# One core, cached attention decode: how P reaches its key partitions before PV

## The chip, the core and the metric

One core of one Trainium2 chip runs the whole program in one launch. The metric is the device time of an execution in microseconds. Beside the timed runs there is one profiled execution, whose trace gives the instructions of each engine: TensorE (PE for matmuls, PEld for its weight loads), VectorE (DVE), ScalarE (ACT), GpSimd (POOL) and SyncE (SP), which issues the DMAs.

## What is computed

Two layers, each an attention block with a cache and a gated feed-forward block, for four tokens (batch 4, one query position). The weights of both layers are the same, and so are the caches.

```
def _A_ref(x, k_cache, v_cache, wq, wo):       # Hq 32, Hkv 8, Sk 4096, Dh 128, D 512
    q = (x @ wq).reshape(B, 1, 32, 128).transpose(0, 2, 1, 3)
    k = jnp.repeat(k_cache, 4, axis=1); v = jnp.repeat(v_cache, 4, axis=1)
    p = softmax(einsum("bhqd,bhkd->bhqk", q, k) * 128 ** -0.5)
    o = einsum("bhqk,bhkd->bhqd", p, v)
    return o.transpose(0, 2, 1, 3).reshape(B, 1, 4096) @ wo
def _B_ref(x, w_gate, w_up, w_down):           # F 1792
    return (sigmoid(x @ w_gate) * (x @ w_up)) @ w_down

x = x + _A_ref(layernorm(x), k_cache, v_cache, wq, wo)
x = x + _B_ref(layernorm(x), w_gate, w_up, w_down)
x = x + _A_ref(...)                            # second layer, as the first
x = x + _B_ref(...)
```

A cache of one batch element and one key/value head is 4096 x 128 bf16, 1 MB; there are 32 of K and 32 of V.

## The kernel before, in words

The unit of work is one (layer, batch, key/value head), with 1 MB of K and 1 MB of V. Two units make a stage, which the code calls g; there are 32 stages, in the order written out in ORDER. The table RET says which K and V stay in SBUF for the second layer. Twelve slots of 1 MB hold K and V; pump() hands the next load to SP's queue whenever a slot is free, in a fixed order (loads). A slot is given back after the last matmul that reads it, so SP's queue waits for TensorE: for the scores (L940) where a K slot is freed, and for PV (L1048) where a V slot is.

The program is written as one list of instructions per engine, in program order. Each instruction carries the semaphore waits that follow from the names it reads and writes. The main loop goes over steps k; step k works on stage sg = k up to its probabilities, and on stage vg = k - 1 for its PV. The order on TensorE within a step is: scores(sg), one wo pair of an earlier stage (do_wo), spread_max(sg), pv of both units of vg, ptrans(sg). Between them stand, at places listed in PLACES, the parts of a batch element's pass: the feed-forward block of layer 0, then layer norm and q of layer 1. DVE transposes K in 32x32 blocks (k_turn, L923) ahead of the scores.

What one stage does around the change:

- scores (L940): 16 matmuls of 512 columns write S in four strips of 32 partitions. A row of S_ps is a head with a part of the keys; 64 of the 128 rows are in use, 512 keys long.
- smax (L956) takes row maxima on DVE, spread_max (L965) brings them to every partition by an fp32 matmul with valid_f as moving operand, and softmax has DVE combine them with a mask (L975, its elementwise output goes to junk and is not used) into one bias per row. ACT then makes the exponentials pe_sb (L983), in bf16, and the row sums.
- ptrans (L1000) turns pe_sb: four matmuls, one for each 128 columns, with pe_sb as weights and 64 selected columns of the identity as moving operand. Keys are then on partitions, but each 32-row strip x of the PSUM tile PT holds, for every a, keys that belong on the partitions of strip a. A matmul with head_f (L1007) sums the row sums, and DVE takes the reciprocal into rden (L1015).
- Sixteen copies (L1032), one for each pair (x, a), each 32 partitions by 64 columns, bring PT into pT_sb on the right partitions. All run on ACT, except that in the last stage half of them run on DVE (L1026).
- pv (L1048): for each unit 32 matmuls with V as 128x128 weights and four columns of pT_sb as moving operand. They come in four groups of eight, one for each x, and a group waits only for the copies of its x.
- normalise (L1080) multiplies by rden; wo_pair (L1098) is 32 matmuls into columns 64 and up of the same PSUM tile O_ps, and DVE adds the result to x (L1112).

There is one buffer each of pe_sb, PT and pT_sb.

Of the kernel before, what the change touches and what calls it, by code (L numbers as in the profile page):

```python
# [5 lines left out]
dt = mybir.dt  # L6
# [179 lines left out]
def bass_interleave_layers__gqa_block_cached__glu_gated_glu__decode_kernel(  # L186
# [17 lines left out]
    P = 128  # L204
# [45 lines left out]
    ident_bf = sbt([P, P], dt.bfloat16, "ident_bf")  # L250
    valid_f = sbt([P, 16 * REP], dt.float32, "valid_f")
    head_f = sbt([P, 2 * REP], dt.float32, "head_f")
    mask_f = sbt([P, 2, 8, REP], dt.bfloat16, "mask_f")
    junk = sbt([P, 16 * REP], dt.bfloat16, "junk")

    row_sb = sbt([P, D], dt.bfloat16, "row")
    x_io = row_sb
# [1 line left out]
    xc_sb = sbt([P, KD, Bn], dt.float32, "xc")  # L259
    sq_sb = sbt([P, KD, Bn], dt.float32, "sq")  # L260
    dn_sb = sq_sb
    newt = sbt([P, 9, Bn], dt.float32, "newt")
    lnsum, lnsq, vpe, nt_a, nt_b, nt_c, nt_y, rs = [newt[:, i, :] for i in range(8)]
    y0i = newt[:, 8, :].bitcast(dt.int32)
    xc_bf = sbt([P, KD, Bn], dt.bfloat16, "xc_bf")
    qT_sb = sbt([P, HQ * Bn], dt.bfloat16, "qT")
    qc_sb = sbt([P, Bn, HKV, NT4, REP], dt.bfloat16, "qc")
    qz_sb = [sbt([P, 2, NT4, 4, REP], dt.bfloat16, f"qz{i}") for i in range(2)]
    oT_sb = [sbt([P, HQ, 2], dt.bfloat16, f"oT{i}") for i in range(2)]
    pe_sb = [sbt([P, 4, P], dt.bfloat16, "pe")] * 2  # L270
    pT_sb = [sbt([P, XJ, 4, 4, REP], dt.bfloat16, "pT")] * 2
    rden_2 = sbt([P, 2, 2 * REP], dt.float32, "rden")
    rden_sb = [rden_2[:, i, :] for i in range(2)]
    pe_f = pe_sb[0].rearrange("p j m -> p (j m)").bitcast(dt.float32)
    iota_f = pe_f[:, 0:P]
    pidx = pe_f[:, P:P + 32]
# [166 lines left out]
    def head_masks():  # L443
        dve(
            lambda e: e.tensor_copy(
                valid_f.rearrange("p (g w) -> p g w", g=4),
                ident_bf.rearrange("p (g w) -> p g w", g=4)[:, :, 0:4 * REP],
            ),
            reads=IDENT,
            writes=["valid"],  # L450
        )
        dve(
            lambda e: e.tensor_tensor(
                half_f[:, :, :], rows_f[:, :, 0, 0:4 * REP], rows_f[:, :, 1, 0:4 * REP], ALU.add
            ),
            writes=["pe0"],
        )
        dve(
            lambda e: e.tensor_reduce(
                head_f.rearrange("p (u h) -> p u h", u=2),  # L460
                half_f.rearrange("p u (a h) -> p u h a", h=REP),
                AX.X,
                ALU.add,
            ),
            reads=["pe0"],
            writes=["head"],
        )
        dve(
            lambda e: e.tensor_scalar(
                mask_f[:, :, :, :],  # L470
                head_f.rearrange("p (u h) -> p u h", u=2).unsqueeze(2).broadcast_to([P, 2, 8, REP]),
                1.0, BIG, op0=ALU.subtract, op1=ALU.mult,
            ),
            reads=["head"],
            writes=["mask"],
        )
        dve(
            lambda e: e.tensor_reduce(rm_sb[0], head_f[:, :], AX.X, ALU.add), reads=["head"], writes=["rm0"]
        )
        dve(  # L480
            lambda e: e.tensor_scalar(rowk_f, rm_sb[0], -exp_scale, None, op0=ALU.mult),
            reads=["rm0"],
            writes=["rowk"],
        )
        dve(
            lambda e: e.tensor_reduce(blk_f, ident_bf.rearrange("p (a c) -> p a c", a=4), AX.X, ALU.add),
            reads=IDENT,
            writes=["blk"],
        )
# [63 lines left out]
    def newton_many(y0, nb):  # L553
        y, yk = y0, "y0i"
        for it, three in enumerate((3.0, 12.0, 768.0)):
            dve(
                (lambda y: lambda e: e.tensor_tensor(nt_a[:, 0:nb], y, y, ALU.mult))(y),
                reads=[yk],
                writes=["nt_a"],
            )  # L560
            dve(
                lambda e: e.tensor_tensor(nt_y[:, 0:nb], nt_a[:, 0:nb], vpe[:, 0:nb], ALU.mult),
                reads=["nt_a", "vpe"],
                writes=["nt_y"],
            )
            z, zk = ((nt_b[:, 0:nb], "nt_b"), (nt_c[:, 0:nb], "nt_c"), (rs[:, 0:nb], "rs"))[it]
            dve(
                (lambda y, z, three: lambda e: e.scalar_tensor_tensor(
                    out=z, in0=nt_y[:, 0:nb], scalar=-three, in1=y, op0=ALU.add, op1=ALU.mult
                ))(y, z, three),  # L570
                reads=[yk, "nt_y"],
                writes=[zk],
            )
            y, yk = z, zk
# [10 lines left out]
    def ln_b_rs(nb):  # L585
# [3 lines left out]
                lnsq[:, 0:nb], M[:, 32:32 + KD * nb].rearrange("p (k b) -> p b k", k=KD), AX.X, ALU.add  # L589
            ),  # L590
            reads=["M1"],
            writes=["lnsq"],
        )
        dve(
            lambda e: e.tensor_scalar(vpe[:, 0:nb], lnsq[:, 0:nb], inv_d, eps, op0=ALU.mult, op1=ALU.add),
            reads=["lnsq"],
            writes=["vpe"],
        )
        dve(
# [361 lines left out]
    def spread_max(g):  # L961
        p = g % 2
        S.inst(
            "pe",
            lambda e: e.matmul(  # L965
                MS[:, 0:16 * REP], lhsT=rm_sb[p].broadcast_to([P, P]), rhs=valid_f[:, :], start=True, stop=True
            ),
            reads=[f"rm{p}", "valid"],
            writes=["MS"],
        )  # L970

    def softmax(g):
        p = g % 2
        dve(
            lambda e: e.tensor_tensor_reduce(  # L975
                junk[:, :], MS[:, 0:16 * REP], mask_f.rearrange("p u n h -> p (u n h)"), rowk_f, BIG,
                ALU.add, ALU.min, nm_sb[p],
            ),
            reads=["MS", "mask", "rowk"],
            writes=["junk", f"nm{p}"],  # L980
        )
        act(
            lambda e: e.activation(  # L983
# [11 lines left out]
    def ptrans(g):  # L995
        p = g % 2
        fns = []
        for j in range(4):
            fns.append(
                (lambda j: lambda e: e.matmul(  # L1000
                    PT[:, j * 64:(j + 1) * 64], lhsT=pe_sb[p][:, j, :], rhs=valid_bf, start=True, stop=True
                ))(j)
            )
        S.group("pe", fns, reads=["pe0"] + IDENT, writes=["PT"])
        S.inst(
            "pe",
# [3 lines left out]
            reads=[f"sm{p}", "head"],  # L1010
            writes=["MS"],
        )
        src = PT[:, 0:256].rearrange("p (j g a h) -> p j g a h", j=4, g=4, h=REP)
        dve(
            lambda e: e.reciprocal(rden_sb[p], MS[:, 64:64 + 2 * REP]),  # L1015
            reads=["MS"],
            writes=[f"rden{p}"],
        )
        late = g == NP - 1
        for x in range(XJ):  # L1020
            for a in range(4):
                dst = pT_sb[p][32 * a:32 * a + 32, x, :, :, :]
                frm = src[32 * x:32 * x + 32, :, :, a, :]
                if late and x % 2:
                    dve(
                        (lambda dst, frm: lambda e: e.tensor_copy(dst, frm))(dst, frm),  # L1026
                        reads=["PT"],
                        writes=[f"pT_{x}" if a == 3 else f"pT_{x}_{a}"],
                    )
                else:  # L1030
                    act(
                        (lambda dst, frm: lambda e: e.activation(dst, frm, ACTF.Copy))(dst, frm),  # L1032
                        reads=["PT"],
                        writes=[f"pT_{x}" if a == 3 else f"pT_{x}_{a}"],
                    )

    def pv(i):
        l, b, u = seq[i]
# [1 line left out]
        p = g % 2  # L1040
        s = where["v", b, u]
        vv = slot[s].rearrange("p (j d) -> p j d", d=DH)
        for x in range(XJ):
            fns = []
            for c in range(2):
                for j in range(4):
                    fns.append(
                        (lambda x, c, j: lambda e: e.matmul(  # L1048
                            O_ps[p][:, ul * REP:(ul + 1) * REP],
                            lhsT=vv[:, x * JG + c * 4 + j, :],  # L1050
                            rhs=pT_sb[p][:, x, j, 2 * ul + c, :],
                            start=(x == 0 and c == 0 and j == 0),
                            stop=(x == XJ - 1 and c == 1 and j == 3),
                        ))(x, c, j)
                    )
            rd = [f"s{s}", f"pT_{x}"] + [f"pT_{x}_{a}" for a in range(3)]
            if ul == 0 and x == 0:
                S.group("pe", fns, reads=rd, writes=[f"O{p}"])
            else:
                S.last_write[f"O{p}"] = S.group("pe", fns, reads=rd)  # L1060
        if l == 1 or not kept("v", i):
            free.append(where.pop(("v", b, u)))

# [9 lines left out]
    def normalise(g):  # L1073
# [4 lines left out]
        held[n, u, c] = (l, b)  # L1078
        dve(
            lambda e: e.tensor_tensor(  # L1080
                oT_sb[n][:, u * REP:(u + 2) * REP, c], O_ps[p][:, 0:2 * REP], rden_sb[p], ALU.mult
            ),
            reads=[f"O{p}", f"rden{p}"],
            writes=[f"oT{n}_{u}_{c}"],
        )

    def wo_pair(g, p):
# [7 lines left out]
        for c in range(KD):  # L1095
            for r in range(2 * REP):
                fns.append(
                    (lambda c, r: lambda e: e.matmul(  # L1098
                        O_ps[p][:, 64 + 2 * c:64 + 2 * c + nb],
                        lhsT=wo_sb[:, u * REP + r, c * P:(c + 1) * P],  # L1100
                        rhs=oT_sb[n][:, u * REP + r, 0:nb],
                        start=(r == 0),
# [1 line left out]
                    ))(c, r)  # L1104
                )
        S.group(
            "pe", fns, reads=[f"oT{n}_{u}_{c}" for c in range(nb)] + [f"wo{u}", f"wo{u + 1}"], writes=[f"O{p}"]
        )
        bs = [b] if pb is None else [b, pb]
        for c, bb in enumerate(bs):  # L1110
# [1 line left out]
                (lambda c, bb: lambda e: e.tensor_tensor(  # L1112
                    xT[:, :, bb],
                    xT[:, :, bb],
                    O_ps[p][:, 64:64 + 2 * KD].rearrange("p (k two) -> p k two", two=2)[:, :, c],
                    ALU.add,
                ))(c, bb),
                reads=[f"x{bb}", f"O{p}"],
                writes=[f"x{bb}"],
            )  # L1120

# [60 lines left out]
    for k, (sg, vg) in enumerate(plan):  # L1182
# [36 lines left out]
        do_steps(k, 6)  # L1219
        if sg is not None:  # L1220
            ptrans(sg)
        do_steps(k, 7)
        if vg is not None and vg in ends:
            close(vg, k)
# [72 lines left out]
```

## Time and profile before

| | |
|---|---|
| median of 3 runs | 326.92 us (325.71 to 328.48) |
| the profiled execution | 326.53 us |
| its span, first to last instruction | 324.7 us |
| mean granted TensorE clock | 0.686 |
| HBM read | 122.95 MB, 379 GB/s over the span |
| ACT copies PT to pT (L1032) | 504, 108.1 us busy |
| matmuls into PT (L1000) | 128, 12.0 us busy |
| PV matmuls (L1048) | 2048, 62.0 us busy |
| V loads | 56 of 1 MB, 11.0 us from issue to landing |
| K loads | 48 of 1 MB, 11.7 us from issue to landing |

How to read it: an engine's busy time says only how much of the span it worked. Lines such as "L1032 ACT ACTIVATE pT<-PT ... x504 | 108.1, 214 | 55.1 <-..." give a group of instructions by source line: output and inputs, shapes, count, busy time in us, mean duration of one in ns, and the engine's idle time before them with what ended it. In a timeline line the first number is the start in us from the start of the span, the second the time from the first start to the last end of the group. "issue" means that an engine stood still without waiting for anything that the profile shows.

### The profile page before, as it was taken

How to read it: one execution, taken by the hardware profiler on the slowest of the kernel's cores; microseconds unless marked ns; L12 is line 12 of the kernel's file. 1: busy time of each engine (PE TensorE's matmuls, PEld its weight loads, DVE VectorE, ACT ScalarE, POOL GpSimd, SP SyncE). 2: the span in 40 equal slices, each digit the busy share in tenths (PEclk: the TensorE clock that was granted, in tenths of full speed). 3: DMA queues.
4: the chain of work that ended last, by engine and by line, in shares of the span. 5: the costliest groups of instructions: out<-in, count | busy, mean ns of one | idle time of the engine just before them, and what ended most of it. 6: DMA issues, size and time to landing. Idle time of an engine off the chain costs nothing.

```text
span 324.7 us, 10428 instructions
## 1 busy us (share of the span) xinstructions
PE 227.0 (70%) x4408; PEld 157.4 (48%) x4408; DVE 188.0 (58%) x441; ACT 145.4 (45%) x600; POOL 12.8 (4%) x36
## 2 busy tenths in 40 slices
PE   1345523008197998768798986799797869878975
PEld 1313312006156465546556564464565646455865
DVE  6387343304656458865647696674886467475243
ACT  1005421205045276655435765543676653377620
POOL 0000000000000010000001000000100000010000
PEclk9999999999996655555765555555655555675555
DMA  7999999999999999999999999999999999999800
GB/s 277 428 422 411 401 404 400 401 386 390 400 406 376 339 376 425 418 422 418 410 370 377 417 424 421 421 388 380 377 421 419 420 422 422 417 416 419 369 18 3
DMA packets 22814, 123.63 MB, mean 381 GB/s; under 512 B 2024, under 2 KB 7920, under 8 KB 8944
## 3 DMA queue, kind: packets, MB, share of 16 engines
q1 hardware_dynamic: 22768, 122.96, 94.1%
q8 instruction: 35, 0.57, 0.7%
q14 instruction: 11, 0.09, 0.1%
HBM read 122.95 MB, written 0.00 MB: 379 GB/s over the span
## 4 chain that ended last, share of the span: by engine, by line
DMA 29%; PE 24%; issue 22%; DVE 12%; SPq 11%; ACT 1%; POOL 0%; DVEq 0%; POOLq 0%
DMA slot<-in_A_v_cache_dram 19%; PE O_ps L1048 7%; DVE slot L923 7%; SPq L382 6%; DMA wo<-in_A_wo_dram 5%; DMA slot<-in_A_k_cache_dram 5%; SPq L368 4%; PE S_ps L940 4%; PE O_ps L1098 3%; PE MS L965 2%; PE MS L1007 2%; PE M_ps L858 1%; DVE small L956 1%; PE M_ps L809 1%; PE PT L1000 1%
## 5 line engine op out<-in xcount | busy, mean ns | idle before, releaser
L1032 ACT ACTIVATE pT<-PT 32x64 bf16<-32x64 f32 x504 | 108.1, 214 | 55.1 <-PE PT L1000 43.6
L923 DVE STREAM_TRANSPOSE slot<-slot 128x2048 f32<-128x2048 f32 (+1 forms) x61 | 112.3, 1840 | 32.4 <-DMA slot<-in_A_k_cache_dram 32.4
L1048 PE MATMUL O_ps<-pT,slot 128*128 128x4 bf16 x2048 | 62.0, 166 | 26.3 <-DMA slot<-in_A_v_cache_dram 26.3
L1048 PEld LDWEIGHTS O_ps<-pT,slot 128*128 128x128 bf16 x2048 | 63.5, 105 | 29.8 <-DMA slot<-in_A_v_cache_dram 27.2
L940 PE MATMUL S_ps<-slot,qz 128*16 128x512 bf16 x512 | 59.4, 612 | 3.4 <-POOL qz L675 2.3
L983 ACT ACTIVATE pe<-S_ps,small 128x512 bf16<-128x512 f32 x32 | 22.0, 686 | 59.0 <-issue 40.4
L965 PE MATMUL MS<-valid_f,small 128*128 128x64 f32 x64 | 20.6, 422 | 22.4 <-DVE small L956 22.4
L1098 PEld LDWEIGHTS O_ps<-oT,wo 128*128 128x128 bf16 x640 | 19.3, 105 | 28.8 <-issue 28.4
L965 PEld LDWEIGHTS MS<-valid_f,small 128*128 128x128 f32 x64 | 15.0, 291 | 37.6 <-DVE small L956 34.1
L1098 PE MATMUL O_ps<-oT,wo 128*128 128x2 bf16 (+1 forms) x640 | 20.3, 166 | 16.7 <-DMA wo<-in_A_wo_dram 15.6
L956 DVE TENSOR_REDUCE small<-S_ps 128x1 f32<-128x512 f32 x32 | 21.2, 662 | 6.5 <-PE S_ps L940 6.5
L675 POOL TENSOR_TENSOR qz<-qc,small 128x128 bf16<-128x128 bf16 x32 | 12.6, 399 | 280.9 <-ACT qc L661 143.5
L940 PEld LDWEIGHTS S_ps<-slot,qz 128*16 128x16 bf16 x512 | 12.4, 109 | 22.8 <-issue 17.7
L1007 PE MATMUL MS<-head_f,small 128*128 128x8 f32 x64 | 17.9, 353 | 0.0
L1080 DVE TENSOR_TENSOR oT<-O_ps,rden 128x8 bf16<-128x8 f32 x32 | 5.2, 164 | 19.7 <-PE O_ps L1048 17.9
L1007 PEld LDWEIGHTS MS<-head_f,small 128*128 128x128 f32 x64 | 16.4, 314 | 0.0
L1015 DVE RECIPROCAL rden<-MS 128x8 f32<-128x8 f32 x32 | 6.6, 206 | 14.8 <-PE MS L1007 14.8
L975 DVE CUSTOM_DVE_ANT_0 junk<-MS,mask_f,small 128x64 bf16<-128x64 f32 x32 | 8.5, 267 | 11.4 <-PE MS L965 11.4
L1000 PE MATMUL PT<-ident_bf,pe 128*128 128x64 bf16 x128 | 12.0, 231 | 1.9 <-ACT pe L983 1.5
L1112 DVE TENSOR_TENSOR xT<-xT,O_ps 128x4 f32<-128x4 f32 x32 | 3.9, 154 | 16.1 <-PE O_ps L1098 16.0
L809 PE MATMUL M_ps<-wq,xc_bf 128*1 128x512 bf16 x128 | 12.9, 574 | 0.0
L661 ACT ACTIVATE qc<-M_ps 128x128 bf16<-128x128 f32 x8 | 1.9, 280 | 19.5 <-PE M_ps L650 19.5
(79 smaller groups left out, 150.3 us busy)
## 6 DMA issues: line engine op xcount, KB each, us to landing
slot<-in_A_v_cache_dram SPq DMA_DIRECT2D x56, 1024.0 KB, 11.0
slot<-in_A_k_cache_dram SPq DMA_DIRECT2D x48, 1024.0 KB, 11.7
wq<-in_A_wq_dram SPq DMA_DIRECT2D x4, 1024.0 KB, 7.8
wo<-in_A_wo_dram SPq DMA_DIRECT2D x8, 512.0 KB, 15.9
wg<-in_B_w_gate_dram SPq DMA_DIRECT2D x4, 448.0 KB, 14.0
wu<-in_B_w_up_dram SPq DMA_DIRECT2D x4, 448.0 KB, 14.4
wd<-in_B_w_down_dram SPq DMA_DIRECT2D x2, 896.0 KB, 16.6
row<-in_A_x_dram SPq DMA_DIRECT2D x1, 4.0 KB
```

The lines of the kernel that those rows point to most:

```text
L382: S.dma("sp", (lambda dst, src: lambda e: e.dma_start(dst, src))(dst, src), f"d{s}", writes=[f"s{s}"])
L809: (lambda k, st: lambda e: e.matmul(M_ps[h][32 * st:32 * st + 1, :], lhsT=xc_bf[:, k, 0:1], rhs=wv[:, k, h, :, st, :], start=(k == 0), sto ...
L923: dve(lambda e: e.transpose(kf, kf), writes=[f"s{st}"])
L940: (lambda t, b2, e_, c, r0, ul: lambda e: e.matmul(S_ps[p][r0:r0 + 4 * REP, :], lhsT=qz_sb[p][:, ul, t, :, :].rearrange("p a r -> p (a r)" ...
L956: lambda e: e.tensor_reduce(rm_sb[p], S_ps[p][:, :], AX.X, ALU.max),
L965: lambda e: e.matmul(MS[:, 0:16 * REP], lhsT=rm_sb[p].broadcast_to([P, P]), rhs=valid_f[:, :], start=True, stop=True),
L983: lambda e: e.activation(pe_sb[p].rearrange("p j m -> p (j m)"), S_ps[p][:, :], ACTF.Exp, bias=nm_sb[p], scale=exp_scale, accum_out=sm_sb[ ...
L1000: (lambda j: lambda e: e.matmul(PT[:, j * 64:(j + 1) * 64], lhsT=pe_sb[p][:, j, :], rhs=valid_bf, start=True, stop=True))(j)
L1007: lambda e: e.matmul(MS[:, 64:64 + 2 * REP], lhsT=sm_sb[p].broadcast_to([P, P]), rhs=head_f[:, :], start=True, stop=True),
L1032: (lambda dst, frm: lambda e: e.activation(dst, frm, ACTF.Copy))(dst, frm),
L1048: (lambda x, c, j: lambda e: e.matmul(O_ps[p][:, ul * REP:(ul + 1) * REP], lhsT=vv[:, x * JG + c * 4 + j, :], rhs=pT_sb[p][:, x, j, 2 * ul ...
L1098: (lambda c, r: lambda e: e.matmul(O_ps[p][:, 64 + 2 * c:64 + 2 * c + nb], lhsT=wo_sb[:, u * REP + r, c * P:(c + 1) * P], rhs=oT_sb[n][:, ...
```

## The change

The turn of P is done in another way. Instead of four matmuls with all 128 columns as weights, there are 64: for each of the four column blocks j, each 32-column piece x and each strip a, a matmul takes 32 columns of pe_sb as weights and 16 columns of the identity (those of the rows that belong to a) as moving operand, and writes straight to strip a of PT. PT then holds P as PV wants it, and one ACT copy of 128x256 brings it to SBUF (pcopy, called right after ptrans). PV is as before with V as weights, but its 32 matmuls of a unit are one group that waits for all of pT.

Beside that: rden has one buffer instead of two; the moving operand of spread_max is read in another order, with mask_f laid out to match; L975's unused output goes to PSUM columns 128 to 191 of MS; wo_pair writes to columns from 384 of O_ps instead of 64 and has a name of its own (W) for its dependences; the layer norm's scratch is smaller.

```
-    mask_f = sbt([P, 2, 8, REP], dt.bfloat16, "mask_f")
-    junk = sbt([P, 16 * REP], dt.bfloat16, "junk")
+    mask_f = sbt([P, 8, 2 * REP], dt.bfloat16, "mask_f")
+    rden_c = sbt([P, 2 * REP], dt.float32, "rden")
...
-    pT_sb = [sbt([P, XJ, 4, 4, REP], dt.bfloat16, "pT")] * 2
+    pT_sb = sbt([P, XJ * 4 * 2, 2, REP], dt.bfloat16, "pT")
...
-                MS[:, 0:16 * REP], lhsT=rm_sb[p].broadcast_to([P, P]), rhs=valid_f[:, :], start=True, stop=True
+                MS[:, 0:16 * REP], lhsT=rm_sb[p].broadcast_to([P, P]),
+                rhs=valid_f.rearrange("p (u n h) -> p n u h", u=2, h=REP), start=True, stop=True
...
-                junk[:, :], MS[:, 0:16 * REP], mask_f.rearrange("p u n h -> p (u n h)"), rowk_f, BIG,
+                MS[:, 128:128 + 16 * REP], MS[:, 0:16 * REP], mask_f.rearrange("p n w -> p (n w)"), rowk_f, BIG,
...
         for j in range(4):
-            fns.append(
-                (lambda j: lambda e: e.matmul(
-                    PT[:, j * 64:(j + 1) * 64], lhsT=pe_sb[p][:, j, :], rhs=valid_bf, start=True, stop=True
-                ))(j)
-            )
+            for x in range(XJ):
+                for a in range(4):
+                    fns.append(
+                        (lambda j, x, a: lambda e: e.matmul(
+                            PT[32 * a:32 * a + 32, (x * 4 + j) * 16:(x * 4 + j) * 16 + 16],
+                            lhsT=pe_sb[p][:, j, 32 * x:32 * x + 32],
+                            rhs=ident_bf.rearrange("p (u c w) -> p c u w", u=2, c=2)[:, :, :, a * REP:(a + 1) * REP],
+                            start=True,
+                            stop=True,
+                        ))(j, x, a)
+                    )
...
-        late = g == NP - 1
-        for x in range(XJ):
-            for a in range(4):
-                dst = pT_sb[p][32 * a:32 * a + 32, x, :, :, :]
-                frm = src[32 * x:32 * x + 32, :, :, a, :]
-                if late and x % 2:
-                    dve(
...
-                else:
-                    act(
...
+    def pcopy(g):
+        act(
+            lambda e: e.activation(
+                pT_sb.rearrange("p n u h -> p (n u h)"),
+                PT[:, 0:256],
+                ACTF.Copy,
+            ),
+            reads=["PT"],
+            writes=["pT"],
+        )
...
-                            rhs=pT_sb[p][:, x, j, 2 * ul + c, :],
+                            rhs=pT_sb[:, (x * 4 + j) * 2 + c, ul, :],
...
-            rd = [f"s{s}", f"pT_{x}"] + [f"pT_{x}_{a}" for a in range(3)]
-            if ul == 0 and x == 0:
+        rd = [f"s{s}", "pT"]
+        if ul == 0:
...
-                        O_ps[p][:, 64 + 2 * c:64 + 2 * c + nb],
+                        O_ps[p][:, 384 + 2 * c:384 + 2 * c + nb],
...
         if sg is not None:
             ptrans(sg)
+            pcopy(sg)
```

## The prediction

> **What bounds the kernel now.** I read the page's engine lines and the 40 slices first, then the DMA queues, the groups by line and form, and last the timeline of the final stages and the chain of waits.
>
> ```profile
> PE 227.0 (70%) x4408; PEld 157.4 (48%) x4408; DVE 188.0 (58%) x441; ACT 145.4 (45%) x600; POOL 12.8 (4%) x36
> PEclk9999999999996655555765555555655555675555
> DMA  7999999999999999999999999999999999999800
> q8 instruction: 35, 0.57, 0.7%
> ```
>
> DMA is busy until 305 of 324.7 us: the stream of K, V and weights sets the pace and no engine is full. So what one stage costs matters only where TensorE is late. Those places show in the rates by window: about 420 GB/s in most of the second half, but 357 in 96 to 112 us, 370 in 164 to 180 and 382 in 212 to 232, each time that a batch's feed-forward pass sits among the attention stages. There slots come free late and the queue runs shallow. From the V that lands at 295.96 us to the end nothing waits for data:
>
> ```profile
> 301.46 0.69 ACT L983 ACTIVATE pe<-S_ps,small 128x512 bf16<-128x512 f32 x1 [0.35 <-ACT pT L1032]
> 302.45 0.38 PE L1000 MATMUL PT<-ident_bf,pe 128*128 128x64 bf16 x4
> 302.64 0.57 PE L1007 MATMUL MS<-head_f,small 128*128 128x8 f32 x2
> 302.92 3.79 ACT L1032 ACTIVATE pT<-PT 32x64 bf16<-32x64 f32 x16 [0.69 <-PE PT L1000]
> 303.14 1.88 PE L940 MATMUL S_ps<-slot,qz 128*16 128x512 bf16 x16
> 304.96 1.01 PE L1098 MATMUL O_ps<-oT,wo 128*128 128x2 bf16 x32
> 305.83 0.68 PE L965 MATMUL MS<-valid_f,small 128*128 128x64 f32 x2
> 306.31 1.89 PE L1048 MATMUL O_ps<-pT,slot 128*128 128x4 bf16 x64
> 308.06 0.37 PE L1000 MATMUL PT<-ident_bf,pe 128*128 128x64 bf16 x4
> ...
> 310.01 0.59 PE L1098 MATMUL O_ps<-oT,wo 128*128 128x2 bf16 x16 [0.77 <-issue]
> ```
>
> This is one dense stage (period 5.61 us, 302.45 to 308.06). TensorE has no gap in it. The sixteen copies (302.92 to 306.71) lie beside scores, wo and spread; PV starts at 306.31 and does not wait for them. Exp waits 0.35 us, and is done at 302.2 against 302.45 when TensorE gets to it. So ACT's 108.1 us of copies are hidden, and what is put on TensorE is not.
>
> The last line is an odd one: in the middle of a group without a semaphore TensorE stands still for 0.77 us. It does so at 126.29 too. In the trace's DMA records the 35 packets of q8 are 16384 bytes each; 2 x 4408 TensorE instructions over 35 is 252 per packet. Counted in order, both stalls fall on a multiple of 256 apart, and each ends 2.4 us after a q8 packet began. So TensorE's program comes in blocks of 256, each asked for when the block before is entered. The second stall's block was entered at 303.96 at the latest and the next was there at 310.01: 6.05 us. After the first stall, 126.75 plus 4.38 until the next packet began plus 2.4 is 6.8. No block went faster than 5.76 us while data flowed (251.12 to 256.88); with DMA idle one took 3.93 (316.12 to 320.05), and with a shallow queue the wait for two packets (171.49, 228.85) puts it near 4.
>
> **The change, part by part.**
>
> *Sixteen copies out, one in.* The page has L1032 at 214 ns x504, and 8 casts of 223 ns on DVE in the last stage. The new copy is 128x256 from PSUM. Nearest rows: 128x128 takes 280 ns (L661), 128x512 takes 595 (L779); between them, 0.39 us. ACT drops by about 3 us a stage. It is worth nothing where PV does not wait for pT. In the last stage the next PV starts at 310.46, behind wo and its 0.77 us stall, and could start up to 0.8 us earlier; if the stall falls there again it gains nothing. I take 0.5.
>
> *Four matmuls out, 64 in, on TensorE's path.* The old group holds TensorE 0.19 us (302.45 to 302.64). The new one has 32 weight columns, 16 moving columns and four column strips in turn. The nearest row is L650, with the same weights' width and the same strips:
>
> ```profile
> 284.87 0.28 PE L650 MATMUL M_ps<-qT,ident_bf 128*32 128x32 bf16 x16
> 285.08 0.29 PE L1000 MATMUL PT<-ident_bf,pe 128*128 128x64 bf16 x4
> ```
>
> Sixteen take 0.28 us with a mean of 176 to 180 ns, so (0.28 - 0.18) / 15 = 6.7 ns each, at clock 1.00; at 0.50 that may be 13.3. 64 x 6.7 = 0.43 us, 64 x 13.3 = 0.85. If the strips did not overlap, PV's row is the bound: 64 in 1.89 us, 27 ns each, 1.7 us. I take 0.65, since the shape is L650's.
>
> The row after L650 starts 0.21 us after it although sixteen matmuls issue in 0.10: leaving the strips costs about 0.1 us. PT now stands between two full-width groups, so two such changes are added, 0.2. [...]
>
> Together 0.65 + 0.2 - 0.19 = 0.66, say 0.6 us a stage; ends 0.25 (0.43, one change hidden) and 1.7. The scores of the next stage, the smax behind the K transpose (DVE waits for the sum L1007 before its reciprocal and the transpose), PV and the release of slots to SP's queue all stand behind it.
>
> *120 more instructions a stage.* Sixty matmuls and their weight loads. A dense stage with wo has 242 to 246 TensorE instructions now, one without 178 to 183, the two stages of a pass about 325 and 413. With 120 more the first needs 1.42 blocks. Ends of the block time: 4 (shallow queue) and 6.8. I take 5.5: nearest to the 5.76 and 6.05, a little under, since a late TensorE leaves the queue shallower. Then a dense stage takes 7.8 us at least (now 5.6 to 6.2, or 6.7 with the 0.6); one without wo 6.4, under its 6.5; pass stages 9.6 and 11.5, under theirs with 0.6 added.
>
> *Small ones.* The spread's rows in another order, junk written to PSUM (L975 is 267 ns; DVE's fill of 512 PSUM columns at L439 takes 485, so 64 columns cost 0 to 0.1 us more), rden in one buffer (normalise precedes the reciprocal on DVE), wo's output under its own key, nt_y dropped: 0, hidden behind TensorE's next group; if not, at most 0.1 us a stage. No DMA is added or moved; SP's and POOL's queues only see later releases. PV's wait for all of pT instead of a quarter: pT is ready about 0.6 us after PT, PV over 3 us after it.
>
> **The sum**, from 100 us on; before that TensorE idles for data up to 15.5 us at a time. Nine dense stages with wo: +1.5 to +2.2 each, 16.6. Four without: 0.6 each, 2.4. Seven pass stages: 0.6 each, 4.3. Six stages that end in a wait for data: little. Together 23.3 us on TensorE's path. V waits of 9.5 us (1.97, 0.52, 3.01, 0.67, 3.00, 0.28) and one K wait of 1.7 take it up, 11.2, so 12.1 are left. The transfers themselves come later through the shallow stretches (I put 6.5 us there: 1, 3 and 2.5), and that moves the V landings with it; TensorE is late by about as much there, so this adds only where the waits would have absorbed more: 1. Less 0.5 in the last stage: +12.6. The profiled execution was 326.53 us (span 324.7, 1.8 around it), close to the median of 326.92; 326.53 + 12.6 = 339.
>
> **The rivals.**
>
> *Fetch stays hidden, TensorE's groups decide.* Then +0.6 a stage: lost in the shallow stretches about 4 us, after 262 us seven stages, 4.2, less 0.28 of slack and 0.8 at the end: +7, 333.5. For it: only two stalls in 35 blocks. Against: many blocks passed with less than 1 us to spare. [...]
>
> *Fully fetch-bound, 6.5 us a block.* A dense stage then takes 9.2 us, +3.2 x 9 = 29; without wo 7.6, +1.6 x 4 = 6; passes 8. 43 less the waits and some drift, 14: +29, 355. Against: the queue would be shallow, and blocks faster.
>
> *Nothing shows.* PT at 0.43 us with one change hidden is 0.25 a stage and waits take it: seven late stages, 1.8, less 0.8: 327.5. It needs blocks under 4.4 us (5.6 + 0.6 over 1.42).
>
> *Faster, through the clock.* The denser TensorE stream could be granted clock 1.00 where it has 0.50. Scores then take 1.04 us instead of 1.88 (the group at 286.03 in the timeline, clock 1.00 there). Three stages at the end save 2.5, and the shallow stretches win back some 5 of the 7 us that their rates lie short of 420 GB/s: 326.5 - 7.5 = 319. It decides once the trace's clock records, which change in steps of 3.4 us, show 1.00 in ordinary stages. Against: 296 to 308 us had TensorE busy 12.00 of 12.00 us at clock 0.50.
>
> **How the numbers follow.** Fetch and groups (339) 0.50; fetch hidden (333.5) 0.20; fully fetch-bound (355) 0.10; nothing shows (327.5) 0.13; clock (319) 0.07. One per cent, 3.3 us, is about what a measurement can tell. Faster: the clock and a hundredth more, 0.08. Same: 327.5 and a little of the second, 0.14. Slower 0.78. The range runs from 328, which leaves out the clock and half of "nothing shows", to 354, which leaves out most of the fetch-bound case.
>
> **What would show it.** Right: the PT matmuls x2048 with 0.5 to 0.9 us per group of 64; one ACT copy of 0.4 us; q8 packets near 50; stops of TensorE inside groups put down to issue, several in the dense stages, whose period is 7 to 8 us. Wrong on fetch: dense stages of 6.2 us without such stops. Wrong on the groups: 64 matmuls over 1.2 us, or the old wait for pT shown to have mattered. Wrong altogether: DMA at 420 GB/s through the passes and an end before 327.

## The result, and the profile after

The changed kernel takes 359.32 us in the median (358.98 to 360.38), the kernel before beside it 326.95: 1.0993 times as long, 95% interval 1.0941 to 1.1046. I had said 339, in a range of 328 to 354. The sign was right; the size was missed by 20 us.

The lines of the page of the changed kernel that answer to those shown of before:

```profile
PE 247.0 (69%) x6328; PEld 173.6 (49%) x6328; DVE 186.5 (52%) x433; ACT 49.7 (14%) x128; POOL 12.8 (4%) x36
...
PEclk9999999999966555555565555556555555655555
DMA  7999999999998999967799999789999999699300
...
q8 instruction: 50, 0.82, 0.9%
```

ACT fell from 145.4 to 49.7 us, and nothing came of it. PE rose by 20.0 us, on 1920 more matmuls. DMA, which was at 9 in every slice but the first and the last ones, now has slices of 6 and 7 in the middle: the stream of K and V is interrupted. The last packet of V ended at 335.6 us; before, at 310.5.

The groups of the page for the turn of P, its copy and PV:

```profile
L1047 PE MATMUL O_ps<-pT,slot 128*128 128x4 bf16 x2048 | 61.6, 166 | 18.5 <-DMA slot<-in_A_v_cache_dram 15.8
...
L1002 PE MATMUL PT<-ident_bf,pe 128*32 128x16 bf16 x2048 | 23.1, 178 | 14.3 <-issue 12.4
...
L1027 ACT ACTIVATE pT<-PT 128x256 bf16<-128x256 f32 x32 | 12.3, 383 | 66.2 <-PE PT L1002 66.2
```

The turn has 14.3 us of idle time before its matmuls, 12.4 of it put down to "issue": TensorE stood still inside the group with nothing to wait for that the profile shows. Two consecutive dense stages (the first has no wo pair) and the start of a third show both costs, in the timeline of the changed kernel (TensorE's matmuls alone; start, length, and in brackets the idle time before and what ended it):

```profile
318.64 0.67 PE L1002 MATMUL PT<-ident_bf,pe 128*32 128x16 bf16 x64
319.24 0.60 PE L1013 MATMUL MS<-head_f,small 128*128 128x8 f32 x2
319.77 1.88 PE L939 MATMUL S_ps<-slot,qz 128*16 128x512 bf16 x16
322.45 0.69 PE L964 MATMUL MS<-valid_f,small 128*128 128x64 f32 x2 [0.80 <-DVE small L955]
322.93 1.89 PE L1047 MATMUL O_ps<-pT,slot 128*128 128x4 bf16 x64
324.75 0.67 PE L1002 MATMUL PT<-ident_bf,pe 128*32 128x16 bf16 x64
325.36 0.60 PE L1013 MATMUL MS<-head_f,small 128*128 128x8 f32 x2
325.88 0.60 PE L939 MATMUL S_ps<-slot,qz 128*16 128x512 bf16 x3
328.98 1.87 PE L939 MATMUL S_ps<-slot,qz 128*16 128x512 bf16 x13 [2.49 <-issue]
...
333.94 0.28 PE L1002 MATMUL PT<-ident_bf,pe 128*32 128x16 bf16 x16
335.01 0.53 PE L1002 MATMUL PT<-ident_bf,pe 128*32 128x16 bf16 x48 [0.79 <-issue]
```

The group of 64 holds TensorE 0.60 us (318.64 to 319.24). Between 325.88 and 328.98 the sixteen score matmuls are torn apart, three ahead of a stop and thirteen behind it; at 335.01 the turn itself is. Counted in order, with the semaphore instructions on TensorE's queue beside the matmuls and weight loads (12791 in all, 50 blocks, beside 50 q8 packets of 16384 bytes), each stop falls where a block of 256 TensorE instructions ends, as the two of before did, and each ends 2.2 to 2.5 us after a q8 packet began. There are 22 stops over 0.3 us, 35.9 us in sum; before there were two, 1.6 us. A stop is counted here from the start of the last instruction of a block to the start of the next one, so it is 0.1 to 0.6 us longer than the idle time in brackets.

The waits of TensorE in the changed kernel from 100 to 350 us, as sum, number and longest:

```profile
PE MS L964 <- DVE small L955: 12.1, 14, 1.3
PE O_ps L1097 <- issue: 10.4, 4, 3.6
PE PT L1002 <- issue: 9.1, 8, 2.6
PE S_ps L939 <- issue: 3.8, 2, 2.5
PE O_ps L1047 <- issue: 2.8, 5, 0.8
...
PE O_ps L1047 <- DMA slot<-in_A_v_cache_dram: 1.2, 1, 1.2
```

and in the kernel before, from 100 to 320 us:

```profile
PE MS L965 <- DVE small L956: 12.4, 14, 1.7
PE O_ps L1048 <- DMA slot<-in_A_v_cache_dram: 11.3, 8, 3.0
```

Read together: the waits for V are gone (11.3 to 1.2 us), the stops have come. A late TensorE frees slots late, so the transfers run late too: SP's queue waits 97.2 us for PV and 91.5 us for the scores to free a slot, where before has 93.3 and 72.3.

### The profile page after: what moved, and what is told of

Its sections match the earlier page's. It is cut to its first block, busy times and chain, and to the rows that moved or that the text cites. A ratio compares the mean times of both kernels' runs of the same rounds, so it can differ in the third digit from the quotient of the medians.

```text
span 357.1 us, 13789 instructions
## 1 busy us (share of the span) xinstructions
PE 247.0 (69%) x6328; PEld 173.6 (49%) x6328; DVE 186.5 (52%) x433; ACT 49.7 (14%) x128; POOL 12.8 (4%) x36
## 2 busy tenths in 40 slices
DMA packets 22826, 123.85 MB, mean 347 GB/s; under 512 B 2024, under 2 KB 7920, under 8 KB 8944
## 4 chain that ended last, share of the span: by engine, by line
PE 43%; DVE 21%; DMA 14%; SPq 10%; issue 10%; ACT 0%; DVEq 0%; ACTq 0%
DVE slot L922 12%; PE O_ps L1047 11%; PE S_ps L939 6%; SPq L381 6%; DMA slot<-in_A_v_cache_dram 6%; PE PT L1002 5%; DMA wo<-in_A_wo_dram 4%; DMA slot<-in_A_k_cache_dram 4%; PE MS L1013 4%; SPq L367 4%; PE MS L964 4%; PE M_ps L808 4%; PE O_ps L1097 3%; DVE small L955 3%; PE M_ps L857 2%
## 5 line engine op out<-in xcount | busy, mean ns | idle before, releaser
L939 PE MATMUL S_ps<-slot,qz 128*16 128x512 bf16 x512 | 61.4, 619 | 4.7 <-issue 3.8
L1002 PE MATMUL PT<-ident_bf,pe 128*32 128x16 bf16 x2048 | 23.1, 178 | 14.3 <-issue 12.4
L1002 PEld LDWEIGHTS PT<-ident_bf,pe 128*32 128x32 bf16 x2048 | 19.2, 102 | 16.0 <-issue 13.2
L1027 ACT ACTIVATE pT<-PT 128x256 bf16<-128x256 f32 x32 | 12.3, 383 | 66.2 <-PE PT L1002 66.2
L1013 PE MATMUL MS<-head_f,small 128*128 128x8 f32 x64 | 19.0, 371 | 0.0
L975 DVE CUSTOM_DVE_ANT_0 MS<-MS,mask_f,small 128x64 f32<-128x64 f32 x32 | 8.8, 276 | 10.9 <-PE MS L964 10.9
```

What stands on the lines that cost most here:

```text
L939: (lambda t, b2, e_, c, r0, ul: lambda e: e.matmul(S_ps[p][r0:r0 + 4 * REP, :], lhsT=qz_sb[p][:, ul, t, :, :].rearrange("p a r -> p (a r)" ...
L1002: (lambda j, x, a: lambda e: e.matmul(PT[32 * a:32 * a + 32, (x * 4 + j) * 16:(x * 4 + j) * 16 + 16], lhsT=pe_sb[p][:, j, 32 * x:32 * x + 32],
L1013: lambda e: e.matmul(MS[:, 64:64 + 2 * REP], lhsT=sm_sb[p].broadcast_to([P, P]), rhs=head_f[:, :], start=True, stop=True),
```

## The experiments

Theory F: TensorE's instructions come in blocks of 256, and the 120 more of each stage run into that supply. Rival T: the turn's time on TensorE itself does it, 64 small matmuls on the path of every stage. F' says that a block takes the same time with or without data traffic, W that a block waits behind a fixed number of data packets. The last three runs set B against R, which their expectations explain. The table has what came out; ratios are to the kernel before on the same chip.

```
kernel              us       ratio [95%]               stops over 0.3 us
small_parts         327.30   1.0005 [0.9967, 1.0044]     none
one_copy            326.67   0.9994 [0.9952, 1.0036]     2,  1.0 us
time_only           329.67   1.0075 [1.0041, 1.0110]     none
few_pv_before       324.72   0.9949 [0.9916, 0.9982]     none
few_pv_after        330.27   1.0107 [1.0047, 1.0167]     6,  7.5 us
half_turn           337.10   1.0328 [1.0269, 1.0386]     8, 11.4 us
after               359.32   1.0993 [1.0941, 1.1046]    22, 35.9 us
double_turn         423.07   (profiled execution)       36, 91.2 us
light_before        290.42   0.8873 [0.8832, 0.8914]     none
light_after         308.65   0.9425 [0.9378, 0.9472]     5,  4.1 us
packets4k_before    333.90   1.0208 [1.0166, 1.0250]     1,  1.1 us
packets4k_after     370.23   1.1333 [1.1293, 1.1374]    24, 43.8 us
packets2k_after     373.08   1.1402 [1.1364, 1.1439]    23, 41.9 us
spread_even         352.36   1.0793 [1.0735, 1.0850]    24, 34.3 us (from 100 us on)
bunched_each        363.14   1.1089 [1.1006, 1.1172]    18, 31.0 us (from 100 us on)
bunched_second      371.74   1.1375 [1.1321, 1.1429]    19, 42.2 us (from 100 us on)
```

**The small parts alone**: the changed kernel with the old turn, copies and PV groups.

```diff
-            for x in range(XJ):
-                for a in range(4):          # 64 matmuls
+            fns.append(... PT[:, j * 64:(j + 1) * 64], lhsT=pe_sb[p][:, j, :], rhs=valid_bf ...)
-            pcopy(sg)
+        (the sixteen copies of before, in ptrans)
```

> The changed kernel with the turn of before put back: four matmuls, sixteen copies, PV in groups by quarter. What is left of the change is one rden buffer, the spread's other row order, the unused output in PSUM, wo's own columns and name, the smaller scratch. Theory F (supply of TensorE's instructions: 120 more a stage, and a block of 256 takes about 6.1 us from being entered until the next is there) and theory T (the turn holds TensorE 0.44 us longer in each stage, and all else follows from that) both say as before, 326 to 328 us. Theory C (one of the small parts or the new wait costs it) says 330 or more.

327.30 against 326.83. The spread's order, junk in PSUM, rden in one buffer and wo's own key cost nothing.

**One copy alone**: the kernel before with one copy in place of sixteen.

```diff
-        for x in range(XJ):
-            for a in range(4):
-                act(... pT[32a:32a+32, x] <- PT[32x:32x+32, a] ...)
+        act(lambda e: e.activation(pT_sb[p] (128x256), PT[:, 0:256], ACTF.Copy), reads=["PT"], writes=["pT"])
```

> The kernel before with its sixteen copies replaced by a single ACT copy of 128x256; the moves between partitions are left out, so P meets the wrong keys. It tells what the sixteen copies are worth by themselves. F and T: hidden, 325 to 327.5 us, the gain 0.5 to 1 us in the last stage at most. Theory C' (ACT's 108 us of copies hold something up): 323 or less.

326.67 against 326.76, though the page's group of copies shrank from 108.1 us to:

```profile
L1019 ACT ACTIVATE pT<-PT 128x256 bf16<-128x256 f32 x32 | 12.3, 384 | 42.4 <-PE PT L1000 42.4
```

96 us less of ACT's work are worth nothing: all of it lay beside TensorE. Each PV group waits for all of pT here too, so that wait costs nothing either.

**TensorE's time without the instructions**: two wide matmuls added to each turn of the kernel before.

```diff
+        for n in range(2):
+            fns.append(lambda e: e.matmul(PT[:, 256:512], lhsT=ident_bf[:, :], rhs=pe_sb[p][:, 0:2, :], ...))
         S.group("pe", fns, reads=["pe0"] + IDENT, writes=["PT"])
```

> The kernel before with two more matmuls of 256 columns in the turn's group, their output unused: about 0.43 us more of TensorE in each stage, with only 4 more instructions. F: the group's time alone, 329 to 335 us, and no stops by issue beyond the two of before. T: the whole loss, 355 to 360.

The page shows the added group:

```profile
L1006 PE MATMUL PT<-pe,ident_bf 128*128 128x256 bf16 x64 | 18.5, 390 | 0.0
```

By my estimate it puts 0.42 us a stage on TensorE's path at clock 0.50 (in the kernel before, score matmuls of 512 columns on one strip start 0.42 us apart, 303.14 to 304.39, and these two have 256 each). That is as much as the new turn adds (0.42, below), with four instructions in place of 120. That cost 2.5 us (0.75%) of the 32. T falls.

**Fewer PV instructions, in both kernels**: one PV matmul of 4 columns and three wide ones in place of 32, so 112 TensorE instructions fewer a stage in about the same time (1.89 us for both units in few_pv_after, 297.67 to 299.56, as the 64 matmuls at 322.93 above).

```diff
-        (32 matmuls of 4 columns for each unit)
+        fns = [1 matmul, rhs=pT (4 columns)] + [3 matmuls, lhsT=vv[:, n, :], rhs=wq_sb[:, 0, 0:w], w = 368, 368, 250]
```

> The changed kernel with PV's 32 matmuls of a unit replaced by one of 4 columns and three wide ones (368, 368 and 250 columns), about the same TensorE time at clock 0.50, with 112 instructions fewer a stage; most of the sum over keys is left out. F: instruction count is back at that of before, so the stops by issue go, and what stays is the turn's time: 327 to 336 us. T: as the changed kernel, 356 to 361. If the wide matmuls bring clock 1.00, both are a few us lower and the control few_pv_before shows it.

> Control: the same replacement of PV in the kernel before (most of the sum over keys is left out). F: 325 to 327.5, since its two stops (0.7 and 0.9 us) go and little else hung on the count. T: 326 to 328.

With the new turn still there the time falls from 359.3 to 330.27, and the page says

```profile
q8 instruction: 36, 0.59, 0.7%
```

36 packets, where before has 35. The control is 0.5% under the kernel before, a little better than expected. So the new turn costs 5.6 us (330.27 against 324.72) where instructions are scarce in the rest of the stage, and 32.4 where they are not. F's time for few_pv_after holds (327 to 336 us), T's does not. The stops did not all go: with about as many instructions as before, few_pv_after still has six, 7.5 us in sum, where before has two, so the count over the program is not all that matters. The granted clock was higher in both profiled executions (0.738 and 0.751, before 0.686), which is why the two are compared with each other.

**Half and twice the turn.**

```diff
-                for a in range(4):        # half_turn: strips 2 and 3 left out, 32 matmuls
+                for a in range(2):
```

```diff
+        (double_turn: the same 64 matmuls once more, into PT[:, 256:512], which nobody reads)
```

> The changed kernel with 32 of the 64 turning matmuls: the turn onto strips 2 and 3 is left out. 56 instructions a stage more than before instead of 120, the group some 0.33 us. F: a dense stage has about 300 instructions, 1.17 blocks, 7.1 us at 6.1 a block: 335 to 345 us, with q8 packets near 43. T: half the loss, 340 to 345. So this run tells the two apart only by where the time lies: F has stops by issue inside groups, 10 to 16 us in all.

> The changed kernel with another 64 turning matmuls a stage whose output is unused: 128 more instructions a stage, 16 more blocks in all, and about 0.43 us more of TensorE. F: 16 blocks at 6.1 us, from 359 to 440 to 460 us, every block boundary a stop. T: 375 to 392.

Added instructions a stage of 0, 56, 120 and 248 give stops of 1.6, 11.4, 35.9 and 91.2 us. The response is not a line. half_turn came out in F's range and under T's; double_turn came out below what F had said, far above T. In its page the second 64 matmuls take as long as the first; the idle time before them is what has grown:

```profile
L1014 PE MATMUL PT<-ident_bf,pe 128*32 128x16 bf16 x2048 | 24.6, 180 | 37.8 <-issue 37.8
...
L1002 PE MATMUL PT<-ident_bf,pe 128*32 128x16 bf16 x2048 | 22.5, 178 | 14.0 <-issue 11.8
```

**Without the data traffic**: K and V loads cut to their first 256 columns, slots filled with zeros once, in both kernels.

```diff
-            dst = slot[s][:, :]
+            dst = slot[s][:, 0:256]
+            src = src[:, 0:256]
```

> The kernel before with every K and V load cut to 64 KB (the rest of each slot is filled with zeros once at the start, which leaves out most of the keys): TensorE's instructions are the same, the data traffic is a sixteenth. F: TensorE sets the pace, 215 to 265 us, and blocks of 256 are there about 3.9 us after the one before was entered.

> The changed kernel with the same cut of the K and V loads (most of the keys are left out). F, if the fetch is slow because of the data traffic: next block after about 3.9 us, a dense stage needs 1.42 blocks, 5.5 us, less than its 6.1 us of work, so no stops and only the group's time: 10 to 18 us above light_before. F', if the fetch takes 6.1 us whatever the traffic: 50 blocks hold it at 290 us or more. T: 14 to 32 us above light_before with no stops.

Both missed. Without its stream the kernel before is only 37 us faster: the chain that ended last, 288.6 us long, has DVE at 39%, TensorE at 36%, issue at 23% and no DMA; I had thought it shorter. The changed kernel loses 18.2 us to its control, a little over F's range and inside T's, and only 4.1 of it are stops; the remaining 14 over 32 stages are 0.44 us each, the group's own time once nothing hides it. The timeline of light_after, TensorE's matmuls again, has dense stages without a stop:

```profile
271.91 0.67 PE L1009 MATMUL PT<-ident_bf,pe 128*32 128x16 bf16 x64
272.51 0.60 PE L1020 MATMUL MS<-head_f,small 128*128 128x8 f32 x2
273.04 1.88 PE L946 MATMUL S_ps<-slot,qz 128*16 128x512 bf16 x16
275.72 0.69 PE L971 MATMUL MS<-valid_f,small 128*128 128x64 f32 x2 [0.80 <-DVE small L962]
276.21 1.89 PE L1054 MATMUL O_ps<-pT,slot 128*128 128x4 bf16 x64
278.03 0.67 PE L1009 MATMUL PT<-ident_bf,pe 128*32 128x16 bf16 x64
```

From 271.91 to 278.03 is 6.12 us, and the group holds 0.60 of it as in the changed kernel. This stage has no wo pair; the one from 284.82 to 290.94, which has one, takes 6.12 us too and has no stop, where the same stage of the changed kernel took 7.05 (from 333.94). In the DMA records the packet of the next block begins 1.1 to 1.9 us after a stop ends and a block is entered; in the changed kernel, behind 15 of the 22 stops, 3.6 to 4.7. So it is the traffic that makes a block late, and F' falls by these waits (its 290 us or more by itself would hold).

**Smaller data packets**: each load split into two or four DMAs of a part of the row, so packets of 4 and 2 KB for 8 (37803 and 67757 packets in all where the changed kernel has 22826).

```diff
-            dst = slot[s][:, :]
+            for h in range(2):
+                dst = slot[s][:, h * 2048:(h + 1) * 2048]
```

> The changed kernel with each 1 MB load of K or V issued as two transfers of half a row each, so that its packets are 4 KB instead of 8 KB; same bytes, order and slots. In the changed kernel a q8 packet starts about 3.8 us after its block was asked for while data flows, 1.1 to 1.4 us where none does. Theory W (it waits behind a fixed number of queued data packets): the wait falls to about 2.5 us, a block to 4.9, most of the 35 us of stops go: 335 to 346 us. Theory B (behind a fixed number of bytes, or for something else): 3.8 us as now, 356 to 362.

> As before it, with four transfers of 2 KB rows. W: the wait near 1.9 us, stops nearly gone, 329 to 340 us unless the smaller packets slow the data itself. B: no better than now, 356 or more.

> Control: the kernel before with 4 KB packets. It has only 1.6 us of stops, so W and B both say 325 to 329 us, unless 4 KB packets carry less, which this run shows (rates below 415 GB/s in the second half).

The wait from entry to packet stayed: 3.76 us in the median with packets of 8 KB, 3.72 with 4, 3.82 with 2. W falls. B's 356 to 362 us was missed as well, by 8 us or more (370.23 and 373.08). The control is 2% slower, which its expectation had left open for packets that carry less. Its page's rates stand at 405 to 409 GB/s for most of the second half, where before has 417 to 424:

```profile
GB/s 279 386 413 400 396 397 397 395 384 382 392 405 357 330 389 408 408 409 407 375 357 361 413 406 409 409 405 388 363 397 411 407 409 408 407 407 408 401 54 2
```

The edit also doubles the number of loads that SP issues, and no run separates that from the packet size.

What the instruction packet waits behind is open. How long it waits goes with the loads that SP had issued and that had not landed when TensorE went on. In the changed kernel these were one behind three of the 22 stops, and the packet began 1.1 to 1.4 us later; two behind three, 1.5 to 3.0 us; three or more behind 16, 2.8 to 4.7 us. The 36 stops of double_turn order the same way: none or one 1.1 to 1.5 us, two 1.4 to 4.0, three or more 3.1 to 4.7.

**The same instructions in other places.** After these runs it was open whether a block takes longer than the 5.5 us of the prediction, or whether charging it by the average of a stage was wrong. Three kernels put 60 tiny matmuls a stage, so 120 instructions, into the kernel before: behind each four scores, as one group in every turn, or as a group of 120 in every second turn.

```diff
+            for n in range(16 if t < 3 else 12):      # spread_even, in scores
+                fns.append(matmul(S_ps[1 - p][32 * (n % 4):32 * (n % 4) + 16, 0:4], lhsT=ident_bf[:, 0:16], rhs=ident_bf[:, 0:4]))
```

```diff
+        for n in range(60):                            # bunched_each, in ptrans; bunched_second: 120 if g % 2 == 1
+            fns.append(matmul(PT[32 * (n % 4):32 * (n % 4) + 16, 256:260], lhsT=ident_bf[:, 0:16], rhs=ident_bf[:, 0:4]))
```

> The kernel before, with 60 tiny matmuls that nobody reads added to every stage (16, 16, 16 and 12 of them behind each four of the sixteen score matmuls): 120 more TensorE instructions a stage, as many as the changed kernel has, placed where TensorE's program is slowest. Two theories of what the 120 instructions cost. B (block by block): only one block of 256 instructions is fetched ahead, so each block that TensorE works through in less than some 5.3 us costs the difference, and a long block pays nothing back. From the trace of before, with 10 ns put in for each added matmul, the blocks then lack 12 to 15 us: 335 to 343 us. R (rate): what counts is how many instructions a stage or a longer stretch has to be supplied with, wherever they stand; then the three kernels of this call, with the same number of instructions, come out within 4 us of each other.

> The kernel before, with the same 60 tiny matmuls in every stage, all of them in one group behind the four matmuls that turn P, where TensorE's program is at its fastest. B (block by block): the blocks lack 20 to 27 us, so 343 to 354 us, and some 10 us more than the kernel with the same matmuls spread. R (rate): within 4 us of the two other kernels of this call.

> The kernel before, with 120 of the tiny matmuls in one group behind the turn of every second stage, none in the others: the same number over the program. B (block by block): the blocks lack 33 to 44 us, so 353 to 369 us, the slowest of the three though the supply over two stages is the same. R (rate): within 4 us of the two other kernels of this call.

All three have 6328 matmuls and 50 packets, as the changed kernel, and they lie 10.8 and 8.6 us apart in the order that B gives: R, which had them within 4 us, falls. Only the second step, from bunched_each to bunched_second, is one of stops and speaks for B; the first is not, as shown below. B's levels were 3 to 9 us too low, taken at the upper ends of its ranges. The view of waits of bunched_second, 100 to 350 us, shows the bunch meeting the end of a block:

```profile
PE PT L1006 <- issue: 21.4, 10, 4.2
PE MS L965 <- DVE small L956: 10.2, 12, 1.2
PE O_ps L1105 <- issue: 10.1, 4, 4.4
```

For all kernels I took the blocks that TensorE enters after 100 us: how long it works through one (waits for semaphores included), and how long after its entry the next one is there (the next q8 packet's start plus 2.39 us, the median from packet to the end of a stop). In the changed kernel exactly one packet begins within each of the 41 blocks, 0.1 to 4.7 us after its entry. I read this as one block asked for when the one before is entered, and no more. "Lack" sums what each block's work falls short of the mean arrival.

```
kernel           blocks  mean work  mean arrival  lack   stops measured
before             28      7.59        5.18        1.3       1.6 us
few_pv_after       29      7.33        5.79        5.9       7.5
half_turn          34      6.32        5.61       12.7      11.4
after              41      5.29        5.26       29.6      31.5
bunched_each       41      5.44        5.44       29.6      31.0
spread_even        41      5.12        5.51       28.0      34.3
bunched_second     42      5.25        5.13       40.9      42.2
double_turn        55      4.20        4.96       77.2      80.3
```

In the changed kernel the mean block brings as much work as the next one needs to arrive (5.29 and 5.26 us). By averages there would be nothing to lose. But its blocks take 2.7 to 9.8 us, and a long one pays nothing back. bunched_each and bunched_second have nearly the same means; doubling the bunch adds 11.2 us of stops. spread_even does not fit this neatly: spreading did not lessen the stops (34.3). My forecast for it had counted the waits of before as a block's work; that these waits turned into stops is argued, not shown. It is faster than bunched_each because 41 blocks hold 0.32 us less each, 13 us; 4.8 of that are waits of spread_max for DVE (11.6 to 6.8 us), the rest I did not settle.

No kernel that computes the reference beat the one before.

## Why the prediction was wrong, point by point

- *ACT's sixteen copies are hidden.* Right: one_copy changes nothing. The new copy takes 383 ns (estimated 0.39 us). So little could be won, and the sign followed.
- *The group of 64, 0.65 us and 0.6 net.* Too high: 0.60 us to the next group's start, where 0.65 and 0.2 for two changes of strips had been summed. Less the old 0.19 it is 0.41, and 0.44 from the pair without traffic; I take 0.42. By itself it is worth about 2.5 us (time_only).
- *The small ones cost nothing.* Right: small_parts.
- *TensorE's program comes in blocks of 256, each asked for when the one before is entered.* It was read from two stalls and 35 packets of before, and the changed kernel agrees: 50 packets, one in each of 41 blocks, and all 22 stops where a block of 256 ends.
- *Block time 5.5 us.* About right as a mean (5.26 over all blocks), with luck. The 5.76 us that it was set by is a block that TensorE worked at for that long; its next packet began 1.9 us after 251.12, so the next block was there after some 4.3. Behind the stops it is 6.15 us in the median (3.76 to the packet, 2.39 more). That a shallower queue makes blocks faster is borne out (3.5 to 3.9 us in four of the 22 stops, with one or two loads still to land), but behind most stops it was not shallow enough.
- *"Then a dense stage takes 7.8 us at least", one without wo 6.4, "under its 6.5", pass stages 9.6 and 11.5, "under theirs".* **This is the step that failed.** It charged 1.42 blocks against a whole stage's time, which lets a long block pay for a short one, and so found 0.9 to 1.6 us in nine stages and nothing in the others: 16.6 less 9 x 0.6, 11.2 us. Charged block by block, the same 5.5 us give 34.9 us on the working times of the changed kernel; 31.5 us were measured, 29.9 more than before. By stages, from one turn to the next, the nine dense ones with wo hold 13.6 of it, not far from the 11.2. The other 17.9 lie where nothing was charged: 10.4 in the pass stages and 7.5 in the stages without wo or with a wait for data. The pass stages hold the longest stops, one of 3.6 us inside wo (285.43 to 288.99), behind a block of 2.7 us that began at 282.69; in the timeline of the changed kernel:

```profile
282.69 1.15 PE L1047 MATMUL O_ps<-pT,slot 128*128 128x4 bf16 x38 [0.83 <-issue]
283.77 0.67 PE L1002 MATMUL PT<-ident_bf,pe 128*32 128x16 bf16 x64
284.37 0.60 PE L1013 MATMUL MS<-head_f,small 128*128 128x8 f32 x2
284.82 0.78 PE L1097 MATMUL O_ps<-oT,wo 128*128 128x2 bf16 x24
289.00 0.37 PE L1097 MATMUL O_ps<-oT,wo 128*128 128x2 bf16 x8 [3.40 <-issue]
```

- *Waits of 11.2 us take it up.* About right: TensorE's V waits fell by 10.1 us. The trace of before has no wait for K of 1.7 us on TensorE or DVE from 95 us on; the wait for data of that size is one for V, which ended at 100.95, and 1.2 us of it stayed. TensorE's waits for qz went from 1.5 us to none.
- *The sum.* With the one term replaced, 339.0 - 11.2 + 29.9 = 357.7. The group at 0.42 in the 20 stages where I charged it takes off 3.6. Two stops end blocks that TensorE entered ahead of 100 us, which I left out. The one of 3.4 us that ended at 79.88 cost nothing, since a wait for V follows it and the turn at 90.5 begins at the same time in both kernels (90.51 and 90.52); the one that ended at 103.31 adds 1.0. That gives 355.1, where the profiled execution took 358.98. Of the 3.9 us between, the group in the six stages that had ended in a wait for data, where I charged little and the waits are gone, would be 2.5; the rest is open. The 29.9 is measured in the changed kernel, so this shows where most of the missing time was, not that it could have been forecast.
- *The rivals.* Fetch hidden (333.5) fell: 22 stops, 35.9 us. "Nothing shows" fell with it. The clock rival fell too: the mean granted clock was 0.67, before 0.69. "Fully fetch-bound" (355, a tenth of the chance) came nearest, though not for its 6.5 us a block in every stage: the mean block was quicker, the blocks were uneven. That it came near is luck. My argument against it, a shallow queue, holds for the mean and not behind most of the stops.

## What to carry to other kernels

Count the instructions of a change on its engine, not only their time: here 120 more of 0.4 us in sum cost 30 us, because TensorE got 256 instructions at a time, one block ahead (one packet in each of 41 blocks), and a block took 5 to 6 us to come (5.26 in the mean, 6.15 in the median behind a stop) beside a stream of 344 GB/s. Charge it block by block, in program order: wherever 256 instructions in a row held less work than that, the difference was lost (29.6 us by that sum, 31.5 measured), and a slow stretch elsewhere did not give it back. In the profile of the changed kernel this is idle time put down to "issue" in the middle of a group, and TensorE goes on 2.2 to 2.5 us after a 16 KB packet of the instruction queue began (all 22 stops).

## What the runs showed of the hardware that was not expected

- A block of TensorE's instructions was slower beside data traffic: 1.1 to 1.9 us from entry to packet without it, mostly 3.6 to 4.7 with it, and 2.2 to 2.5 more until TensorE goes on (the 22 stops of the changed kernel). The size of the data packets (8, 4, 2 KB) did not change the median wait (3.76, 3.72, 3.82 us); it goes with the number of loads still to land (one 1.1 to 1.4 us, two 1.5 to 3.0, three or more 2.8 to 4.7).
- Loads split in two, with packets of 4 KB, carried 405 to 409 GB/s, those of 8 KB 417 to 424; the kernel before lost 2% by it. Whether the packet size or the doubled number of loads does it was not separated.
- 64 matmuls of 32 weight columns, in four column strips in turn, take 0.60 us, 9.4 ns each, at clock 0.50 (318.64 in the changed kernel, 271.91 in light_after).
